# A fused attention and MLP kernel: the order of MLP units in the gaps between attention bursts, and the start of the first four units

## The chip, the cores and the metric

The kernel runs on one core of one Trainium2 chip. A core has TensorE (PE, matmuls), ScalarE (ACT), VectorE (DVE), GpSimd (POOL) and SyncE (SP, which here only issues transfers). Matmul results lie in PSUM, operands in SBUF, inputs and outputs in device memory. The metric is the device time of one launch in microseconds; lower is better.

## The reference

Attention with normalised queries and keys over 8 batches, 12 heads, 448 positions and 64 values per head; then a two-layer MLP (768 to 2048 to 768) over the 3,584 tokens with a leaky activation that has one slope per hidden column:

```python
def rmsnorm(x, g):
    return x / sqrt(mean(x * x, axis=-1) + 1e-06) * g
scores = (rmsnorm(q, g_q) @ rmsnorm(k, g_k).T) / sqrt(64)
attn = exp(scores - max(scores))
attn = attn / (sum(attn) + 1e-09)
x = (attn @ v) with the heads side by side        # 3584 x 768
h = x @ w_in
g = maximum(h, 0) + alpha * minimum(h, 0)
out = g @ w_out
```

The kernel takes a constant bias of -8 in the exponent in place of the maximum. It computes the activation as the larger of `h` and `alpha * h`, which is the same for slopes between 0 and 1.

## The kernel before

**Tiles and stages.** The unit of attention is a group `y` of four heads; a batch has three (G = 3), so there are 24. Its work in order:

- `load_qk` brings q and k into `nat` (on SP, from six buffers, so three groups); `square` (on POOL from group 2), `reduce` (DVE, tile `ss`), `root` (ACT, a logarithm and an exponential, tile `rr`) and `scale` (POOL, and DVE for a few, tile `qs`) normalise them.
- `turn` puts head values on the partitions: on PE through the tile `tps` for groups below 8, with DVE copies to `qT` and `kT`; from group 8 a transposing DMA does it, and `turn` is one DVE multiplication.
- `score` is four 64 by 64 matmuls into a tile `sc` of two PSUM banks (pool `pss`, two tiles). `soft` is an ACT exponential of the tile (1.0 us alone, about 0.94 in a row) into `expT`. Seven of each make a group.
- `den` sums the exponentials in 28 matmuls (tile `dn`); `log` and `invert` on ACT make the inverse (`rden`); `attv` takes 28 matmuls with the values (`av`), and a DVE multiplication writes one third of the batch's `xT`. `dn` and `av` share the pool `psa`, one tile with the tag `acc`.

The MLP is cut into units. `up(b, ft)` makes 128 of the 2,048 hidden columns of a batch: six matmuls over two halves of three thirds of `xT`, then ACT writes `ah` (alpha times h) and DVE the larger of both to `gT`. `down(b0, t, oh)` makes half of the output columns of 128 tokens of a pair of batches: 16 matmuls over all `gT`, a DVE copy to `osb`, and, after the second half, two output transfers on SP. Both write single banks of `psf` (two banks, tag `mm`), or half of the `acc` tile when `spare` is set. `spin(count)` gives PE matmuls whose result nobody reads.

**Order.** Every engine works in the order in which the program issues; the code writes that order. A small planner (lines 335 to 435) divides the work into 66 bursts of two or three score tiles. `dens` and `avs` say in which burst a group's denominators and values stand, `turn_at` where it is turned, `roots` where it is normalised, and `prep`, `post` and `jobs` where loads, squares and reduces stand. The MLP units of a batch are spread over the next batch's bursts (`gaps`), by a running sum of assumed costs (1.13 us for `up`, 2.6 for `down`); `old` are `down` units carried over, `new` those of this pair of batches.

Before, unit order in a gap is: the first of a burst from `old` while there is one, then `up`, and at the end `new`. One unit per burst, behind the first, may use the spare tile. The first MLP units stand in burst 12, together with the values of group 2, after a burst 11 with its denominators:

```python
        lead = n in (den_at[G - 1], av_at[G - 1])
        if lead and n in dens:
            den(dens[n])
            log(dens[n])
            invert(dens[n])
        elif lead:
            attv(avs[n])
```

`spin` fills PE ahead of the first units: after the scores in bursts 0, 1, 3 and 10, and in bursts 11 and 12. The weights come on POOL's queue: `w_in` in four parts in bursts 0 to 6, `w_out` in four parts, one each in bursts 10 to 13.

Of the kernel before, what the change touches and what calls it, by code (L numbers as in the profile page):

```python
# [9 lines left out]
FP32 = mybir.dt.float32  # L10
# [11 lines left out]
def kernel(  # L22
# [12 lines left out]
    nc = tc.nc  # L35

    B, H, S, D = q.shape
# [193 lines left out]
            scale=QK_SCALE, bias=expb[:, 0:1],  # L231
        )

    def over_keys(name, y, weights):
        acc = psa.tile([128, 2, 512], FP32, name=name, tag="acc")
        e = expT[y]
        for j in range(J):
            for g in range(2):
                for par in range(2):
                    nc.tensor.matmul(  # L240
                        out=acc[ds(64 * par, 64), g, :S],
                        lhsT=weights(g, par, j),
                        rhs=e[ds(64 * g, 64), j, par, :],
                        start=(j == 0),
                        stop=(j == J - 1),
                    )
        return acc
# [11 lines left out]
        r = rden[y]  # L259
        nc.scalar.activation(out=r, in_=r, func=AF.Exp, scale=-1.0)  # L260

    def attv(y):
        b, i = divmod(y, G)
        vv = vt[b]
        av = over_keys("av", y, lambda g, par, j: vv[ds(64 * g, 64), 2 * i + par, j, :])
        if i == 0:
            xT[b] = att.tile([128, 2, G, S], FP16, name="xT", tag="xT")
        nc.vector.tensor_mul(  # L268
            out=xT[b][:, :, i, :], in0=av[:, :, :S], in1=rden[y]
        )  # L270


    def bank(name, spare):
# [2 lines left out]
            return t[:, 0]  # L276
        return psf.tile([128, 512], FP32, name=name, tag="mm")

    def up(b, ft, spare=False):
        x = xT[b].rearrange("p g i c -> p (g i) c")  # L280
        hT = bank("hT", spare)
        order = [g * G + i for i in range(G) for g in range(2)]
        for c in order:
            nc.tensor.matmul(  # L284
                out=hT[:, :S],
                lhsT=w_in_sb[:, c, ts(ft, 128)],
                rhs=x[:, c, :],
                start=(c == order[0]),
                stop=(c == order[-1]),
            )  # L290
        ah = ffn.tile([128, S], FP16, name="ah", tag="ah", bufs=3)
        nc.scalar.activation(out=ah, in_=hT[:, :S], func=AF.Copy, scale=alpha_sb[:, ft : ft + 1])  # L292
        nc.vector.tensor_max(out=gT[:, ft, ds((b & 1) * S, S)], in0=hT[:, :S], in1=ah)  # L293
# [43 lines left out]
    while m < NG * J or len(avs) < NG:  # L337
        n = len(bursts)
        if len(dens) > len(avs):
            avs[n] = len(avs)  # L340
        elif len(dens) < NG and last_in.get(len(dens), n) < n:
            dens[n] = len(dens)
        wide = n in dens and dens[n] >= G or n in avs and avs[n] >= G
        count = min(3 if wide else 2, NG * J - m)
        bursts.append([divmod(m + c, J) for c in range(count)])
        for y, j in bursts[n]:
            first_in.setdefault(y, n)
            if j == J - 1:
                last_in[y] = n
        m += count  # L350
# [11 lines left out]
    turn_at = {  # L362
        y: max(n for n in range(first_in[y]) if n not in dens) for y in range(1, NG)
    }
    turn_at[2] = av_at[0] + 1
    turns = {n: y for y, n in turn_at.items()}
    jobs = {}
    for y in range(G, NG):

        early = y < G + 2  # L370
        n = turn_at[y - 1] if early else max(d for d in dens if d <= turn_at[y] - 2)
        at(n - (8 if early else 5), load_qk, y)
        for nm in "qk":
            (after if early else at)(n - 2, square, y, nm)
            if early:
                after(n, reduce, y, nm)
            else:
                jobs.setdefault(n, []).append((reduce, (y, nm)))
        roots[n + 1] = y
    for b in range(1, B):  # L380
        at(av_at[G * b] - 4, load_v, b)

# [2 lines left out]

    periods, carry = [], []
    for b in range(B):
        ups = [(UP, up, (b, ft)) for ft in range(NF)]
        odd = b % 2
        new = [  # L390
            (DOWN, down, (b - odd, t, oh))
            for t in (range(3, J) if odd else range(3)) for oh in range(2)
        ]
        tail = len(new) if b == B - 1 else 2 if odd or b == 0 else 1
        periods.append((ups, carry, new[:tail]))
        carry = new[tail:]

    def cost(n):
        return (
            0.31 + 0.19 * len(bursts[n])  # L400
            + (1.35 if n in dens or n in avs else 0.0) + (0.9 if turns.get(n, TD) < TD else 0.0)
        )

    first = av_at[G - 1]
    gaps = [[] for _ in range(NB)]
    for b in range(B - 1):
        lo, hi = av_at[G * b + G - 1], av_at[G * b + 2 * G - 1]
        ups, old, new = (list(u) for u in periods[b])
        mlp = sum(u[0] for u in ups + old + new)
        per = (mlp + sum(cost(n) for n in range(lo, hi))) / (hi - lo)  # L410
        clock = 0.0
        for n in range(lo, hi):
            clock += cost(n)
            free = True
            while ups or old or new:
                if old and (free or not ups):
                    u = old.pop(0)
                elif ups:
                    u = ups.pop(0)
                else:  # L420
# [63 lines left out]
    for n in range(NB):  # L484
# [13 lines left out]
        plain = n not in dens and n not in avs  # L498
        wait = plain and gaps[n] and gaps[n][0][0] is up
        if lead and n in avs:  # L500
            spin(3)
        for t in tiles[:1] if wait else tiles[:2]:
            soft(*t)
        if n in dens and not lead:
# [21 lines left out]
                late = [(1, invert, (dens[n],))]  # L526
        done = 0

        spare_at, clock = None, 0.0
        for k, (f, a) in enumerate(gaps[n][:-1]):  # L530
            free = 2.3 if n in dens else 1.2 if n in avs else 0.1
            if spare_at is None and clock >= free and not turns.get(n, TD) < TD:
                spare_at = k
            clock += DOWN if f is down else UP
        for k, (f, a) in enumerate(gaps[n]):
            spare = k == spare_at
# [53 lines left out]
```

## Time and profile before

| What | us |
|---|---|
| Median of 9 runs | 453.92 |
| Lowest and highest | 453.13 and 456.49 |
| The profiled execution, its time | 455.64 |
| Span of its records | 453.9 |
| PE, ACT, DVE, POOL busy | 427.6, 290.0, 207.8, 171.1 |
| First matmul of the MLP starts | 48.30 |

The profile is one execution. Its page gives busy time of each engine, the span in 40 slices, the transfers, the chain of work that ended last and the costliest groups of instructions. A group's line names the code line, the engine, the operation, the tile written and those read, the count, the busy time and the mean of one. Other views list who waited for whom, sum up stretches of time, or give the instructions in order of time; a bracket in the last gives the idle time of the engine ahead and what ended it.

### The profile page before, as it was taken

The numbers are of one execution on the slowest core, as the hardware profiler recorded it, in microseconds if no ns is written. First come the engines' busy times: TensorE is split into PE (matmuls) and PEld (weight loads), VectorE is DVE, ScalarE is ACT, GpSimd is POOL, SyncE is SP. The second block draws the span as 40 slices with busy tenths as digits, with TensorE's granted clock in tenths as the row PEclk, the third lists the DMA queues.
The fourth block names the chain that finished last, engine by engine and source line by source line (L and its number), as shares of the span: only waits on it lengthen the run. The fifth ranks groups of instructions, "written<-read, shape, count | busy, mean of one in ns | idle before, by whom it ended". The sixth has DMA issues, their size and how long they took to land.

```text
span 453.9 us, 9099 instructions
## 1 busy us (share of the span) xinstructions
PE 427.6 (94%) x3848; PEld 230.1 (51%) x3848; DVE 207.8 (46%) x297; ACT 290.0 (64%) x401; POOL 171.1 (38%) x125
## 2 busy tenths in 40 slices
PE   6768989899999999999999999999999999999996
PEld 2333444455445555455545555455545555455563
DVE  2755454735364545345454535345564333343421
ACT  4997888568676757648786758658785847423300
POOL 4779944660570550750571450750541100000000
PEclk9998999999999999999999999999999999999999
DMA  8999995294657633665656632674352410111122
GB/s 190 228 239 242 236 241 119 34 177 124 141 79 158 157 76 83 109 159 143 135 106 136 157 82 77 114 162 136 77 92 46 77 37 1 35 36 36 35 71 69
DMA packets 60009, 52.77 MB, mean 116 GB/s; under 512 B 32688, under 2 KB 56512, under 8 KB 59968
## 3 DMA queue, kind: packets, MB, share of 16 engines
q1 hardware_dynamic: 47424, 39.27, 36.5%
q0 software_dynamic: 11808, 11.81, 16.6%
q10 hardware_dynamic: 736, 1.11, 1.0%
q8 instruction: 30, 0.49, 0.5%
q14 instruction: 11, 0.09, 0.1%
HBM read 45.62 MB, written 11.01 MB: 125 GB/s over the span
## 4 chain that ended last, share of the span: by engine, by line
PE 79%; ACT 14%; DVE 4%; DMA 1%; issue 1%; SPq 0%; ACTq 0%
PE op L301 31%; PE hT L284 18%; PE hTa L284 9%; ACT expT L229 8%; PE sc L217 7%; PE av L240 5%; PE dn L240 5%; ACT ah L292 2%; PE opa L301 2%; ACT rden L255 2%; DVE gT L293 2%; DMA nat<-in_k_dram 1%; ACT rden L260 1%; PE tps L193 1%; DVE ss L141 1%
## 5 line engine op out<-in xcount | busy, mean ns | idle before, releaser
L229 ACT ACTIVATE expT<-sc,expb 128x896 f16<-128x896 f32 x168 | 157.6, 1008 | 19.0 <-PE sc L217 18.8
L301 PE MATMUL op<-w_out_sb,gT 128*128 128x384 f16 x848 | 145.9, 326 | 2.1 <-DVE gT L293 2.0
L158 POOL TENSOR_TENSOR qs<-nat,rr 128x896 f16<-128x896 f32 x44 | 78.3, 1799 | 180.3 <-issue 159.0
L284 PE MATMUL hT<-xT,w_in_sb 128*128 128x448 f16 x558 | 117.1, 353 | 2.7 <-DVE gT L293 2.6
L301 PEld LDWEIGHTS <-gT 128*128 128x128 f16 x896 | 84.6, 98 | 65.5 <-issue 12.3
L284 PEld LDWEIGHTS <-w_in_sb 128*128 128x128 f16 x768 | 73.7, 98 | 72.8 <-issue 8.5
L292 ACT ACTIVATE ah<-hT,cols 128x448 f16<-128x448 f32 x93 | 59.1, 636 | 59.5 <-PE hT L284 59.3
L293 DVE TENSOR_TENSOR gT<-hT,ah 128x448 f16<-128x448 f32 x93 | 58.0, 624 | 76.5 <-ACT ah L292 76.5
L135 POOL TENSOR_TENSOR sq<-nat 128x896 f32<-128x896 f32 x44 | 73.0, 1681 | 1.0 <-DMA nat<-in_q_dram 1.0
L313 DVE COPY osb<-op 128x384 f32<-128x384 f32 x53 | 29.5, 557 | 89.4 <-PE op L301 89.4
L217 PE MATMUL sc<-qT,kT 64*64 64x448 f16 x672 | 53.4, 360 | 9.6 <-ACT expT L229 6.0
L292 ACT ACTIVATE ah<-hTa,cols 128x448 f16<-128x448 f32 x35 | 22.2, 633 | 49.5 <-PE hTa L284 49.5
L141 DVE TENSOR_REDUCE ss<-sq 128x14 f32<-128x896 f32 x48 | 49.9, 1077 | 7.2 <-ACT sq L133 6.8
L284 PE MATMUL hTa<-xT,w_in_sb 128*128 128x448 f16 x210 | 45.4, 352 | 0.0
L217 PEld LDWEIGHTS <-kT 64*64 64x64 f16 x672 | 19.2, 104 | 39.1 <-issue 29.0
L240 PE MATMUL av<-expT,vt 64*64 64x448 f16 x672 | 36.0, 350 | 2.2 <-ACT rden L255 2.2
L240 PE MATMUL dn<-expT,ones 64*64 64x448 f16 x672 | 36.6, 354 | 0.2 <-DVE gT L293 0.2
L268 DVE TENSOR_TENSOR xT<-av,rden 128x896 f16<-128x896 f32 x24 | 26.2, 1090 | 22.3 <-PE av L240 22.3
L293 DVE TENSOR_TENSOR gT<-hTa,ah 128x448 f16<-128x448 f32 x35 | 21.8, 623 | 31.3 <-ACT ah L292 31.3
L240 PEld LDWEIGHTS <-vt 64*64 64x64 f16 x672 | 20.3, 107 | 14.3 <-issue 3.7
L240 PEld LDWEIGHTS <-ones 64*64 64x64 f16 x672 | 20.7, 108 | 12.7 <-issue 2.1
L255 ACT ACTIVATE rden<-dn 128x896 f32<-128x896 f32 x24 | 22.3, 930 | 2.9 <-PE dn L240 2.9
(37 smaller groups left out, 134.4 us busy)
## 6 DMA issues: line engine op xcount, KB each, us to landing
out_dram<-osb SPq DMA_DIRECT2D x54, 192.0 KB, 2.7
nat<-in_q_dram SPq DMA_DIRECT2D x46, 224.0 KB, 5.8
nat<-in_k_dram SPq DMA_DIRECT2D x46, 224.0 KB, 6.9
vt<-in_v_dram POOLq DMA_DIRECT2D x16, 336.0 KB, 7.3
w_in_sb<-in_moe_w_in_dram POOLq DMA_DIRECT2D x4, 768.0 KB, 13.4
w_out_sb<-in_moe_w_out_dram POOLq DMA_DIRECT2D x4, 768.0 KB, 15.6
nat<-in_q_dram ACTq DMA_DIRECT2D x2, 224.0 KB, 4.6
nat<-in_k_dram ACTq DMA_DIRECT2D x2, 224.0 KB, 6.7
```

What stands on the lines that cost most here:

```text
L135: nc.gpsimd.tensor_mul(out=sqf, in0=src, in1=src)
L141: nc.vector.tensor_reduce(out=ss_t[y][:, "qk".index(nm)].rearrange("p h j -> p (h j)").unsqueeze(2), in_=sqs[y, nm], axis=AXIS_X, op=ALU.add,)
L158: eng.tensor_mul(out=t.rearrange("p j h d -> p h j d"), in0=nat[y, nm], in1=rr_t[y][:, "qk".index(nm)].unsqueeze(3).broadcast_to((128, 2, ...
L217: nc.tensor.matmul(out=sc[ds(64 * g, 64), par, :S].rearrange("p (j c) -> p j c", j=J), lhsT=kT[ds(64 * par, 64), j, g, :], rhs=qT[ds(64 * ...
L229: nc.scalar.activation(out=expT[y][:, j], in_=scs[y, j][:, :, :S], func=AF.Exp, scale=QK_SCALE, bias=expb[:, 0:1],)
L240: nc.tensor.matmul(out=acc[ds(64 * par, 64), g, :S], lhsT=weights(g, par, j), rhs=e[ds(64 * g, 64), j, par, :], start=(j == 0), stop=(j == ...
L255: nc.scalar.activation(out=r, in_=rden[y][:, :, :S], func=AF.Ln)
L284: nc.tensor.matmul(out=hT[:, :S], lhsT=w_in_sb[:, c, ts(ft, 128)], rhs=x[:, c, :], start=(c == order[0]), stop=(c == order[-1]),)
L292: nc.scalar.activation(out=ah, in_=hT[:, :S], func=AF.Copy, scale=alpha_sb[:, ft : ft + 1])
L293: nc.vector.tensor_max(out=gT[:, ft, ds((b & 1) * S, S)], in0=hT[:, :S], in1=ah)
L301: nc.tensor.matmul(out=op[:, :OH], lhsT=gT[:, ft, ts(t, 128)], rhs=w_out_sb[:, ft, ds(oh * OH, OH)], start=(ft == 0), stop=(ft == NF - 1),)
L313: nc.vector.tensor_copy(out=o[:, ds(oh * OH, OH)], in_=op[:, :OH])
```

## The change

Five things change, all in the order of work or in the PSUM tiles.

1. The values of group 2 move from burst 12 into burst 11, directly behind its denominators, and go to a score tile (`spare`), while the logarithm and the inverse are issued between its matmuls and the multiplication. MLP units start in burst 11.
2. Units 0 to 3 of batch 0 are cut in two. `begin` sums the first two thirds of `xT`: unit 0 in burst 10 between its scores, 1 to 3 in burst 11 around the scores; 2 and 3 lie in the halves of the `acc` tile (`hTb`). `up` then adds the last third. The `spin` calls of bursts 10, 11 and 12 go; burst 6 gets one, as it no longer has a turn.
3. Group 2 is turned in burst 5, behind the values of group 0, instead of in burst 6; group 4 is normalised in burst 11 instead of 10. The `w_out` parts move one burst earlier each.
4. In a gap, carried `down` units stand first only in bursts with denominators or values (`wide`) as long as there are enough of those; other bursts get `up` units. Batch 0 takes four of its `down` units in its own period instead of two. In the plan that results, bursts 16 to 18 hold four `down` units of batch 0 (before, burst 18 holds two, and burst 16 has `up` units); bursts 31, 46 and 61 hold six `up` units each; and bursts 34, 49 and 64, which before have `up` units and then a `down` of the new pair, hold two `down` units, the carried one first.
5. Every third unit behind the first free place may use the spare tile, where before one per burst could. A PE turn stands behind the second unit of a burst where the burst has more than two.

```diff
-    def over_keys(name, y, weights):
-        acc = psa.tile([128, 2, 512], FP32, name=name, tag="acc")
+    def over_keys(name, y, weights, spare=False):
+        pool, tag = (pss, "sc") if spare else (psa, "acc")
+        acc = pool.tile([128, 2, 512], FP32, name=name, tag=tag)
...
-    def attv(y):
+    def attv(y, spare=False, jobs=()):
         b, i = divmod(y, G)
         vv = vt[b]
-        av = over_keys("av", y, lambda g, par, j: vv[ds(64 * g, 64), 2 * i + par, j, :])
+        av = over_keys(
+            "av", y, lambda g, par, j: vv[ds(64 * g, 64), 2 * i + par, j, :], spare
+        )
+        for f in jobs:
+            f(y)
...
+    begun = {}
+
+    def up_part(hT, b, ft, lo, hi):
+
+        for i in range(lo, hi):
+            for g in range(2):
+                nc.tensor.matmul(
+                    out=hT[:, :S],
+                    lhsT=w_in_sb[:, g * G + i, ts(ft, 128)],
+                    rhs=xT[b][:, g, i, :],
+                    start=(i == 0 and g == 0),
+                    stop=(i == G - 1 and g == 1),
+                )
+
+    def begin(ft):
+
+        if ft < 2:
+            begun[ft] = bank("hT", False)
+        elif ft == 2:
+            t = psa.tile([128, 2, 512], FP32, name="hTb", tag="acc")
+            begun[2], begun[3] = t[:, 0], t[:, 1]
+        up_part(begun[ft], 0, ft, 0, G - 1)
+
     def up(b, ft, spare=False):
...
+        early = b == 0 and ft in begun
+        hT = begun[ft] if early else bank("hT", spare)
+        up_part(hT, b, ft, G - 1 if early else 0, G)
...
             dens[n] = len(dens)
-        wide = n in dens and dens[n] >= G or n in avs and avs[n] >= G
-        count = min(3 if wide else 2, NG * J - m)
+            if dens[n] == G - 1:
+                avs[n] = G - 1
+        three = n in dens and dens[n] >= G or n in avs and avs[n] >= G
+        count = min(3 if three else 2, NG * J - m)
...
-    turn_at[2] = av_at[0] + 1
+    turn_at[2] = av_at[0]
...
-        n = turn_at[y - 1] if early else max(d for d in dens if d <= turn_at[y] - 2)
+        n = turn_at[y - 1] + (y == G) if early else max(d for d in dens if d <= turn_at[y] - 2)
...
-        roots[n + 1] = y
+        roots[n + 1 + (y == G + 1)] = y
...
-        ups = [(UP, up, (b, ft)) for ft in range(NF)]
+        ups = [(UP / 3 if b == 0 and ft < 4 else UP, up, (b, ft)) for ft in range(NF)]
...
-        tail = len(new) if b == B - 1 else 2 if odd or b == 0 else 1
+        tail = len(new) if b == B - 1 else 4 if b == 0 else 2 if odd else 1
...
+    def wide(n):
+        return n in dens or n in avs
...
-                if old and (free or not ups):
+                if old and (not ups or free and (
+                    wide(n) or len(old) > sum(wide(c) for c in range(n, hi))
+                )):
                     u = old.pop(0)
...
-        lead = n in (den_at[G - 1], av_at[G - 1])
-        if lead and n in dens:
+        lead = n == den_at[G - 1]
+        if lead:
             den(dens[n])
-            log(dens[n])
-            invert(dens[n])
-        elif lead:
-            attv(avs[n])
+            attv(avs[n], True, (log, invert))
         for t in tiles[:2]:
             score(*t)
-        plain = n not in dens and n not in avs
-        wait = plain and gaps[n] and gaps[n][0][0] is up
-        if lead and n in avs:
-            spin(3)
+            if lead and t == tiles[0]:
+                begin(1)
+                begin(2)
+            elif n == den_at[G - 1] - 1 and t == tiles[0]:
+                begin(0)
+        plain = lead or n not in dens and n not in avs
+        wait = plain and not lead and gaps[n] and gaps[n][0][0] is up
+        if lead:
+            begin(3)
...
-            if spare_at is None and clock >= free and not turns.get(n, TD) < TD:
-                spare_at = k
+            if clock >= free and not turns.get(n, TD) < TD and (
+                not spare_at or k - spare_at[-1] > 2
+            ):
+                spare_at.append(k)
...
-            if k == 0 and n in turns:
+            if n in turns and k == (
+                0 if turns[n] >= TD or plain else max(min(1, len(gaps[n]) - 2), 0)
+            ):
                 turn(turns[n])
...
-        if n < first and plain and n not in turns:
+        if n < den_at[G - 1] - 1 and plain and n not in turns:
             spin(4)
-        elif lead and n in dens:
-            spin(8)
```

More of the change, by code (lines that the diff above doesn't have):

```diff
@@ L277, in bank @@
         return psf.tile([128, 512], FP32, name=name, tag="mm")
-    def up(b, ft, spare=False):
[L280 to L290, printed above, removed]
+    begun = {}
[16 more added lines that the diff above has]
+        up_part(begun[ft], 0, ft, 0, G - 1)
+    def up(b, ft, spare=False):
+        early = b == 0 and ft in begun
+        hT = begun[ft] if early else bank("hT", spare)
+        up_part(hT, b, ft, G - 1 if early else 0, G)
         ah = ffn.tile([128, S], FP16, name="ah", tag="ah", bufs=3)
@@ L527 @@
         done = 0
-        spare_at, clock = None, 0.0
+        spare_at, clock = [], 0.0
         for k, (f, a) in enumerate(gaps[n][:-1]):
             free = 2.3 if n in dens else 1.2 if n in avs else 0.1
-            if spare_at is None and clock >= free and not turns.get(n, TD) < TD:
-                spare_at = k
+            if clock >= free and not turns.get(n, TD) < TD and (
+                not spare_at or k - spare_at[-1] > 2
+            ):
+                spare_at.append(k)
             clock += DOWN if f is down else UP
         for k, (f, a) in enumerate(gaps[n]):
-            spare = k == spare_at
+            spare = k in spare_at
             if f is down:
```

## The prediction

> **What bounds the kernel now.** I read the page's busy table and slices first, then windows by stage, then the waits, then the timeline of the stretch that the diff rewrites.
>
> ```profile
> PE 427.6 (94%) x3848; PEld 230.1 (51%) x3848; DVE 207.8 (46%) x297; ACT 290.0 (64%) x401; POOL 171.1 (38%) x125
> ...
> PE   6768989899999999999999999999999999999996
> ...
> PEclk9998999999999999999999999999999999999999
> DMA  8999995294657633665656632674352410111122
> ```
>
> TensorE (PE) sets the end; its idle slices are nearly all in the first eight (a slice is 11.35 us). One slice has a reduced clock. DMA is full for six slices, to about 70 us.
>
> ```profile
> 24.00:39.80 15.80, 9.98 (x157) 5.60 (x157) 9.32 (x11) 14.38 (x20) 14.07 (x9) 0.99 1.18 234
> 39.80:48.30 8.50, 8.34 (x92) 3.66 (x88) 4.63 (x5) 6.16 (x9) 8.48 (x8) 0.82 1.17 250
> 48.30:87.50 39.20, 36.26 (x347) 19.36 (x345) 20.07 (x29) 29.49 (x43) 22.25 (x16) 1.00 0.74 158
> 87.50:135.30 47.80, 44.42 (x431) 23.39 (x430) 23.58 (x33) 35.45 (x49) 24.83 (x18) 1.00 0.64 128
> 135.30:450.00 314.70, 311.13 (x2689) 169.92 (x2688) 138.88 (x204) 187.87 (x259) 87.31 (x57) 1.00 0.43 94
> ```
>
> Columns: stretch, length, then PE, weight loads, DVE, ACT, POOL. To 39.8 ACT is the limit (14.38 of 15.80). From 39.8 to 48.3 PE looks full, ACT is not (6.16 of 8.50), and the clock is 0.82. Then PE leaves 2.9 us idle to 87.5, 3.4 to 135.3, 3.6 in the remaining 315.
>
> ```profile
> 39.78 1.67 PE L328 MATMUL spin<-idle,ident 128*128 128x448 f16 x4
> 41.39 2.22 PE L240 MATMUL dn<-expT,ones 64*64 64x448 f16 x28
> 43.66 0.92 ACT L255 ACTIVATE rden<-dn 128x896 f32<-128x896 f32 x1 [1.80 <-PE dn L240]
> 43.92 1.69 PE L328 MATMUL spin<-idle,ident 128*128 128x448 f16 x8
> 45.53 1.52 PE L240 MATMUL av<-expT,vt 64*64 64x448 f16 x28
> 47.17 1.09 DVE L268 TENSOR_TENSOR xT<-av,rden 128x896 f16<-128x896 f32 x1 [3.72 <-PE av L240]
> 47.72 0.74 PE L328 MATMUL spin<-idle,ident 128*128 128x448 f16 x3
> ```
>
> The "full" PE is partly idle work: 15 spin matmuls. The denominators took 2.22 us at half clock against 1.49 to 1.52 elsewhere. Values come only after the logarithm, so the first MLP matmul is at 48.30.
>
> ```profile
> 187.79 2.44 PE L284 MATMUL hT<-xT,w_in_sb 128*128 128x448 f16 x12
> 191.25 0.97 PE L301 MATMUL op<-w_out_sb,gT 128*128 128x384 f16 x5 [1.01 <-DVE gT L293]
> ```
>
> Here `down` directly follows the last two `up` units and waits for what they write.
>
> [...] The records have a half-clock window, 39.44 to 42.85, but the window before it held some 1.8 us of matmuls, [...] The trace shows about 0.1 us per change (from a `down`'s first matmul to the next instruction group it is 2.69 us where scores follow, 2.61 where an `up` does); the change keeps nearly all of these. [...] w_out parts take 15.6 us to land in the full stretch.
>
> **The change, part by part.** Prices: `up` 1.14 us (six matmuls), `down` 2.61, denominators or values 1.32, two score tiles 0.4; exponential 0.94 in a row; ah 0.64; gT 0.62; a root pair 0.55; logarithm 0.92; inverse 0.95; xT 1.09; reduce 1.04.
>
> *Turn of unit 2 one burst earlier.* It then stands behind the values of unit 0 (end 26.9) instead of behind burst 6's scores (28.44). Its k part needs POOL's scale, which ends at 27.16. kT ends at about 29.3 instead of 30.25, and the 0.88 us that ACT idled at 30.75 for scores goes. Worth 0.9 us, as ACT is the limit there.
>
> *Burst 10 to 12.* Spins: 15 removed here, four added in burst 6, where PE idles. Unit 2's values go straight behind its denominators into a score tile, and four `up` units begin on the two finished thirds of xT (4 of 6 matmuls, 0.75 us each). With the 0.9: first part 37.3 to 38.05, inside the wait for kT (0.99 idle before); denominators 38.75 to 40.1, full clock; values to 41.45; log 40.3 to 41.2; inverse to 42.15; xT 42.25 to 43.3. The second score of burst 11 needs the values' tile and waits for that xT: 43.35. Third begin to 44.4. The four remainders (0.38 each) end at 45.9. Before, none of these four was complete until 49.5.
>
> *A wait that the change adds.* Unit 5's reduces now stand behind five gT on DVE. ACT: exponential to 44.7, root to 45.25, four ah to 47.8, the fifth 47.95 to 48.6; gT to 49.3; two reduces to 51.4. Root 5 is in ACT's queue ahead of ah 5, the next exponential and ah 6 to 8, so ACT stands from 49.55 to 51.4, and `up` 8 waits for a bank to 53.25: 1.7 us on PE. Before, these reduces ended by 43.5 with no MLP on DVE.
>
> *Bursts 13 to 18, by the same walk.* Burst 13's scores 54.4, burst 14's 59.9; burst 15: scores 64.2, values to 65.95, 1.55 waiting for an exponential, turn 5 behind xT at 70.4 (both waits are there before, 0.79 and 1.12), `up` 15 to 72.4. Then two `down` per pair of bursts: 73.0 first `down`, burst 19's first score at about 88.2. Before, that score is at 87.51 with 16 `up` and two `down` done; now four `down` are done: 2 x 2.61 - 0.7 = 4.5 us ahead.
>
> *Weights.* The last quarter of w_out is issued at about 52 instead of 55.9 and needed at the 13th matmul of the first `down`, 75. Before it landed at 71.83. All loads are the same bytes, so nothing, with 3 us of cover. But POOL now issues three w_out parts and two v loads in a row ahead of unit 4's scales, which end about 49 instead of 46.45; turn 4 needs them at 56.7, so nothing again.
>
> *Batch 1 (bursts 19 to 26).* Fewer `down` are left, so ACT comes close: bursts 22 to 25 need 20.9 us of PE and 21.8 of ACT (11 exponentials, 9 ah, two log pairs, two roots). Walked with two banks: `up` 7 waits 1.1, `up` 10 1.5, `up` 13 0.6; before, bursts 24 and 25 lose 0.85, 0.32 and 0.77, plus some hidden in the stream, 2.4 in all. Of the 4.5 about 0.6 is given back: 3.9.
>
> *Later batches.* `down` first in bursts 34 and 49 removes a wait of 1.1 (1.01 in the lines above) twice; in burst 64 about 0.55. The spare tile for every third unit removes about 0.4 each in bursts 31 and 46, and moving three units in a row without it to 36 and 51 gives it back. Sum 2.75. The new place of the PE turns changes nothing: bursts 15, 18 and 20 have two units, for which the rule gives index 0, and burst 13 is plain. Rest list and end are untouched.
>
> Sum 3.9 + 2.75 = 6.65 us. The profiled execution took 455.64 with a span of 453.9, so 1.7 lies around it: span 447.25, time 449.0. But it is 1.72 above the median of the runs, which gives 447.3 if the median run has the same half-clock window. I take 448.0 between the two.
>
> **Rivals.** (B) *ACT gives back more.* From 48.3 to 87.5 ACT idles only 9.7 us and my walk spends over half. In-order waits like root 5's, one more per burst in bursts 11 to 15 and 22 to 25, would cost 0.4 each, 3.6: 451.6. For it: ACT interleaves three kinds of work there; against: the walk has them in order. (C) *Half clock again.* [...] 1.6 us a window (0.85 on the spins, 0.75 on the denominators before), 449.6 with one. [...] (D) *Hidden anyway*: the early start only lengthens waits at turn 5 and `down`, the later 2.75 remaining: 451.2. (E) *Slower: the last quarter of w_out.* If five issues in a row block POOL until earlier parts land, squares, scales and the last w_out issue all slip. Each us past 75 is a us on PE; it decides at 75 + 6.65 + 1.4 = about 83. Landing takes 16.2 at most, so an issue at 67 would be needed; two w_in issues in a row did not block. (F) The benefit is larger: bursts 11 to 15 overlap better, root 5's wait absent: 446.
>
> **How the numbers follow.** A measurement can tell about 0.3%, 1.36 us: faster below 452.56, slower above 455.28. Chances: forecast 0.48 (446.3 to 449.5), F 0.10, C 0.12, B 0.12, D 0.08, E or several waits together 0.10 of which 0.07 passes 455.28. Faster takes forecast, F, C, most of B and D: 0.86; same 0.07; slower 0.07. The range leaves out the top of E, part of B and D, and the best of F: 445.0 to 451.8.
>
> **What would show it.** Right: denominators and values of unit 2 adjoining near 39 to 41.5; first complete gT near 46; ACT idle before root 5 by about 1.8 us, released by DVE; burst 19 after four `down` near 88; no PE wait for gT ahead of `down` at bursts 34 and 49. Wrong: `down` waiting on the w_out load, a second 0.5 clock stretch, PE waits for gT above 3 us in batch 1, or ACT idle for scores after 45.

## The result, and the profile after

The changed kernel takes 449.68 us (median; 449.44 to 450.10), the kernel before, run beside it on the same chips, 453.76 us. The ratio is 0.9904, 95% interval 0.9889 to 0.9918: faster by about 4.1 us, or 1.0%. The forecast was 448.0 with a range of 445.0 to 451.8.

The profiled execution after the change took 449.5 us with a span of 447.7. Its busy table and slices (each digit a tenth of a slice of 11.2 us):

```profile
PE 424.6 (95%) x3837; PEld 229.3 (51%) x3837; DVE 207.7 (46%) x297; ACT 290.4 (65%) x401; POOL 171.2 (38%) x125
...
PE   8779798989889999999999999999999999999996
...
PEclk9999999999999999999999999999999999999999
DMA  8999995285547651883666651872362501111122
```

Three things differ from before. TensorE loses 3.0 us of busy time, which is spin matmuls and matmuls at the reduced clock, not work. The slice with the reduced clock is gone. And slices 11 and 12 of TensorE (from 112 to 134 us) stand at 8, because units of batch 1 wait there.

The same windows by stage, after (length, then busy PE, weight loads, DVE, ACT, POOL; clock; transfer share; GB/s):

```profile
24.00:39.80 15.80, 12.97 (x200) 7.48 (x203) 10.49 (x12) 14.94 (x19) 15.45 (x10) 1.00 1.17 244
39.80:48.30 8.50, 6.68 (x55) 3.02 (x46) 3.09 (x5) 6.08 (x10) 8.30 (x9) 1.00 1.18 237
48.30:87.50 39.20, 35.93 (x356) 19.59 (x356) 21.00 (x30) 28.23 (x40) 20.87 (x14) 1.00 0.75 163
87.50:135.30 47.80, 43.14 (x437) 22.58 (x438) 24.35 (x34) 36.28 (x51) 25.49 (x18) 1.00 0.61 128
```

From 87.5 to 135.3 TensorE is now idle for 4.7 us where it was 3.4. That is where part of the gain goes. Here are its three waits in batch 1 (bursts 23, 24 and 26; start, length, instruction; in brackets the idle time ahead and what ended it), and then the two that stood there before (the second profile of the kernel before, from the first experiment below):

```profile
113.98 1.29 PE L290 MATMUL hT<-xT,w_in_sb 128*128 128x448 f16 x6 [0.67 <-DVE gT L313]
...
120.68 1.30 PE L290 MATMUL hT<-xT,w_in_sb 128*128 128x448 f16 x6 [1.01 <-DVE gT L313]
...
128.02 0.38 PE L217 MATMUL sc<-qT,kT 64*64 64x448 f16 x4 [1.34 <-DVE kT L179]
```

```profile
118.91 2.65 PE L284 MATMUL hT<-xT,w_in_sb 128*128 128x448 f16 x12 [0.85 <-DVE gT L293]
...
126.72 1.29 PE L284 MATMUL hT<-xT,w_in_sb 128*128 128x448 f16 x6 [0.76 <-DVE gT L293]
```

The timeline of the start, after:

```profile
37.93 1.49 PE L241 MATMUL dn<-expT,ones 64*64 64x448 f16 x28
...
39.25 1.49 PE L241 MATMUL av<-expT,vt 64*64 64x448 f16 x28
39.48 0.92 ACT L256 ACTIVATE rden<-dn 128x896 f32<-128x896 f32 x1 [0.31 <-PE dn L241]
...
41.41 1.09 DVE L273 TENSOR_TENSOR xT<-av,rden 128x896 f16<-128x896 f32 x1 [1.76 <-ACT rden L261]
...
45.01 1.16 DVE L313 TENSOR_TENSOR gT<-hT,ah 128x448 f16<-128x448 f32 x2 [2.51 <-ACT ah L312]
...
46.75 0.54 PE L290 MATMUL hTb<-xT,w_in_sb 128*128 128x448 f16 x2 [1.82 <-DVE gT L313]
```

Denominators and values adjoin, at a granted clock of 1.00, and the first two `gT` are written by 46.2. The last line is a wait that the forecast did not have. A little later, ACT's timeline of the changed kernel:

```profile
49.05 1.00 ACT L229 ACTIVATE expT<-sc,expb 128x896 f16<-128x896 f32 x1
51.83 0.32 ACT L152 ACTIVATE rr<-ss,epsb 128x28 f32<-128x28 f32 x1 [1.78 <-DVE ss L141]
52.18 0.23 ACT L153 ACTIVATE rr<-rr 128x28 f32<-128x28 f32 x1
52.31 0.62 ACT L312 ACTIVATE ah<-hT,cols 128x448 f16<-128x448 f32 x1
```

This is root 5 in ACT's queue, waiting for the reduces that stand behind five `gT` on DVE. It was forecast, and it holds up an `up` unit on TensorE for 1.20 us at 53.64. The waits view of the new kernel, three lines of it (who waited for whom: total, times, longest):

```profile
PE hT L290 <- DVE gT L313: 3.5, 6, 1.2
...
PE hTb L290 <- DVE gT L313: 1.8, 1, 1.8
...
PE sc L217 <- DVE kT L179: 1.3, 1, 1.3
```

And burst 34, where `down` waited 1.01 us before, is one stream of two `down` units (the first of the 32 matmuls lies ahead of this view):

```profile
183.74 5.20 PE L321 MATMUL op<-w_out_sb,gT 128*128 128x384 f16 x31
```

**Where the 4 us come from.** Times from the start of the span shift with the first loads (ACT's wait for the first k tile was 1.84 us in the first profile of before and 0.78 after), so stretches are compared from one common event: the first matmul of the values of group 0, at 24.15 to 25.79 us in the profiles used here. The work up to there is the same in all of them, so this spread is not an effect of any edit. The rows give the time from there to the first score of a burst, or to the end of the records. At bursts 28, 35, 50 and the end, all kernels have done the same work; at burst 19 the kernel marked with a star has done two `down` (5.22 us) more than before; at burst 13 it has done nine `up` units, the kernel before three, so its larger figure there is not a loss. "Before, again" is the unchanged kernel in the second profile that the first experiment gives.

| us from the values of group 0 to | burst 13 | burst 19 | burst 28 | burst 35 | burst 50 | end |
|---|---|---|---|---|---|---|
| before, first profile | 26.85 | 62.16 | 117.31 | 168.59 | 270.18 | 428.52 |
| before, again | 25.27 | 60.57 | 115.72 | 167.00 | 268.59 | 426.92 |
| after * | 30.33 | 63.25 | 114.63 | 164.34 | 264.92 | 423.19 |

Against "before, again", the change has 5.22 - 2.68 = 2.54 us in hand at burst 19 and 1.09 at burst 28: batch 1 gives back 1.45. It then gains 1.57 to burst 35 and 1.01 to burst 50, and 0.06 to the end: 3.73 in all. The profiled pair that the forecast started from shows more, 453.9 - 447.7 = 6.2 us of span, because the first profile of before has 1.6 us more in the same stretch and came to the common event 0.81 us later (25.35 against 24.54).

### The profile page after: what moved, and what is told of

It reads as the page before. It is cut to its first block, busy times and chain, and to the rows that moved or that the text cites. A ratio compares the mean times of both kernels' runs of the same rounds, so it can differ in the third digit from the quotient of the medians.

```text
span 447.7 us, 9084 instructions
## 1 busy us (share of the span) xinstructions
PE 424.6 (95%) x3837; PEld 229.3 (51%) x3837; DVE 207.7 (46%) x297; ACT 290.4 (65%) x401; POOL 171.2 (38%) x125
## 4 chain that ended last, share of the span: by engine, by line
PE 81%; ACT 11%; DVE 5%; DMA 1%; issue 1%; ACTq 0%
PE op L321 32%; PE hT L290 18%; PE hTa L290 9%; PE sc L217 7%; ACT expT L229 6%; PE dn L241 6%; PE av L241 6%; ACT ah L312 2%; PE opa L321 2%; DVE gT L313 2%; PE tps L193 1%; DMA nat<-in_k_dram 1%; DVE ss L141 1%; ACT rden L256 1%; ACT rden L261 1%
## 5 line engine op out<-in xcount | busy, mean ns | idle before, releaser
L290 PE MATMUL hT<-xT,w_in_sb 128*128 128x448 f16 x528 | 112.1, 353 | 3.5 <-DVE gT L313 3.5
L312 ACT ACTIVATE ah<-hT,cols 128x448 f16<-128x448 f32 x88 | 55.7, 634 | 62.9 <-PE hT L290 62.7
L313 DVE TENSOR_TENSOR gT<-hT,ah 128x448 f16<-128x448 f32 x88 | 54.8, 624 | 61.3 <-ACT ah L312 61.2
L290 PE MATMUL hTa<-xT,w_in_sb 128*128 128x448 f16 x228 | 49.3, 352 | 0.0
L312 ACT ACTIVATE ah<-hTa,cols 128x448 f16<-128x448 f32 x38 | 24.1, 633 | 37.6 <-PE hTa L290 37.6
L313 DVE TENSOR_TENSOR gT<-hTa,ah 128x448 f16<-128x448 f32 x38 | 23.7, 625 | 33.8 <-ACT ah L312 33.8
L261 ACT ACTIVATE rden<-rden 128x896 f32<-128x896 f32 x24 | 22.9, 953 | 0.7
```

The source lines that it names most:

```text
L290: nc.tensor.matmul(out=hT[:, :S], lhsT=w_in_sb[:, g * G + i, ts(ft, 128)], rhs=xT[b][:, g, i, :], start=(i == 0 and g == 0), stop=(i == G ...
```

## The experiments

The question was which of the five parts earns the time, and where the rest of the forecast 6 us went. The theory was the forecast's: a sum of local gains, about 4 us by the early start together with the four `down` units up to burst 19, and 2.75 us by the order later on. The rivals were the half clock, a hidden early start, and queueing behind DVE or the transfers.

### The kernel before, unchanged

> The kernel before, unchanged, to see the granted clock of many executions beside their times. If the half-clock window of the profiled execution (39.44 to 42.85 us) is what set it 1.9 us above the median of 453.76, then executions with a mean clock of 1.0 take about 453.3 and those with one window near burst 10 or 11 about 455 to 456.5, and the gain over a usual execution is 4.1 although the two profiled ones differ by 6.2. Rival: the window costs nothing in the end (ACT or the transfers set the pace there); then times do not go with the clock, and the 1.9 us lie around the span.

Measured: 453.68 us, ratio 1.0001 (0.999 to 1.0012); the profiled execution took 453.39 with a span of 451.6. Its timeline at the denominators and values of group 2:

```profile
39.85 1.52 PE L240 MATMUL dn<-expT,ones 64*64 64x448 f16 x28
41.42 0.92 ACT L255 ACTIVATE rden<-dn 128x896 f32<-128x896 f32 x1 [0.21 <-PE dn L240]
43.30 1.52 PE L240 MATMUL av<-expT,vt 64*64 64x448 f16 x28
...
46.06 2.43 PE L284 MATMUL hT<-xT,w_in_sb 128*128 128x448 f16 x12
```

The denominators take 1.52 us, not 2.22, and the MLP starts at 46.06, not 48.30. So the granted clock of 0.50 that I had seen here (39.44 to 42.85) belongs to that execution and not to every execution of the program. It cost 1.6 us (62.16 - 60.57); the rest of the difference between the two profiles is the start, 25.35 against 24.70. The clocks of the 22 executions of this run say the same. Eleven have a mean granted clock of 0.999 or more and take 453.28 to 454.09 us (median 453.43); seven at 0.995 or 0.996 take 453.30 to 455.25; four at 0.991 or 0.992 take 454.81 to 456.26. So times do go with the clock in this run, and against the median of the eleven an execution took from nothing to 1.8 us more at 0.995 or 0.996, and 1.4 to 2.8 more at 0.991 or 0.992. Such stretches lift the median of this kernel by about 0.3 us, not by the 1.6 of the first profile. The changed kernel at a mean clock of 1.000 takes 449.50 to 449.98 us (median 449.69): at full clock the gain is about 3.7 us, as in the table above.

### The early start alone, with the unit order of before

Parts 1, 2, 3 and 5 stay; with this order no burst has a second spare place.

```diff
-        tail = len(new) if b == B - 1 else 4 if b == 0 else 2 if odd else 1
+        tail = len(new) if b == B - 1 else 2 if odd or b == 0 else 1
...
-                if old and (not ups or free and (
-                    wide(n) or len(old) > sum(wide(c) for c in range(n, hi))
-                )):
+                if old and (free or not ups):
```

> Parts 1, 2, 3 and 5 of the change with the unit order of before. My account: the early start is worth about 3 us over a usual execution by burst 19, and the later waits of before (bursts 24, 25, 34, 49, 64) stay: 450.8, ratio 0.9935. Rival, the early start is hidden (ACT limits bursts 11 to 16, so that what starts early waits later) and nearly all of the gain is in the order: 453 or more, ratio over 0.998.

Measured: 453.24 us, ratio 0.9985 (0.9971 to 0.9999), almost nothing. From the values of group 0 it needs 60.36 us to burst 19 and 426.74 to the end, 0.2 less than before at both. The expectation fell. TensorE's timeline of this kernel shows what stands where the early start should have shown:

```profile
54.40 0.38 PE L217 MATMUL sc<-qT,kT 64*64 64x448 f16 x4 [1.13 <-ACT expT L229]
...
65.18 1.51 PE L241 MATMUL av<-expT,vt 64*64 64x448 f16 x26 [1.38 <-DMA vt<-in_v_dram]
...
85.41 0.57 PE L217 MATMUL sc<-qT,kT 64*64 64x448 f16 x8 [1.31 <-DVE kT L204]
```

TensorE comes sooner to an exponential, to the values of batch 1 and to the `kT` of burst 19, and waits there: 3.8 us in these three, where the kernel before, in its second profile, waits for two exponentials (0.79 each) and a turn (1.12), 2.7 us. With the smaller ones and the 1.82 us that `hTb` costs here too, the lead is gone. My reading is that starting early pays only if there is TensorE work that needs none of these; the new order in batch 0 alone, below, puts it to the test.

### The new unit order alone

The kernel before with only the two edits above in the other direction (the `wide` rule and four `down` units of batch 0 in its own period); the late start and one spare place stay.

> Part 4 of the change alone: the order of units, with the start of before and one spare place per burst. My account: the waits at bursts 34, 49 and 64 go (2.75 us), but the runs of six units in bursts 31, 46 and 61 have one spare place and lose about 0.9 us each, and batch 1 loses about as much as it gains: 453.5, ratio 0.9995. Rival, the order is worth its 2.75 us by itself: 451.0, ratio 0.994.

Measured: 453.27 us, ratio 0.9989 (0.9976 to 1.0001). From the values of group 0 to the end: 426.56 us, 0.36 less than before. TensorE no longer waits for `gT` ahead of a `down`, and from burst 28 to 35 it takes 50.11 us against 51.28. But it is 1.06 us late at burst 28. At burst 19 it is still 0.40 ahead (counting the two `down` that it has done more); batch 1, with less `down` work carried into it, then takes 1.46 away, by the same three waits that the changed kernel has (0.67, 1.02 and 1.34 us here). So the loss in batch 1 is the price of the new order, with or without the early start.

So the parts are not additive: 0.2 and 0.4 us alone, 3.7 together. The next two experiments show where the difference lies.

### The new order in batch 0 only

```diff
-                    wide(n) or len(old) > sum(wide(c) for c in range(n, hi))
+                    b > 0 or wide(n) or len(old) > sum(wide(c) for c in range(n, hi))
```

> The changed kernel with the unit order of before from batch 1 on; batch 0 keeps the new order with four of its second-layer units in bursts 16 to 18. My account: the early start is worth something only where units that need no ACT fill the PE time that it frees, so here it is worth about 2.5 us by burst 19 although the early start alone brought 0.6 and the order alone 0.5; the later waits stay: 451.5, ratio 0.995. Rival, the parts simply add up: 453.0 or more, ratio over 0.998.

Measured: 453.53 us, ratio 0.9989 (0.9979 to 0.9999). The expectation was right up to burst 19 and fell behind it. Up to there the kernel is the changed one to the hundredth (63.25 us), so it has the 2.54 us in hand, where the start alone has 0.21 and the order alone 0.40: with `down` units to do, the early start pays. It then loses 1.04 us against it to burst 28 (115.67 against 114.63), 1.57 more to burst 35 and 1.01 to burst 50. In batch 1 TensorE waits for `gT` or `kT` four times (1.01, 0.76, 1.01, 1.34), in the changed kernel three times (0.67, 1.01, 1.34): the difference of 1.1 us is the 1.04. The 2.54 us in hand at burst 19 are thus spent in batch 1, down to 0.05. With the new order there as well, where carried `down` units are kept for the bursts with denominators and values, 1.09 are left. The later batches' 2.6 us come from that order too (with its second spare place, next), and not from the start: here both waits of 1.0 us ahead of `down` are back.

### One spare place per burst

```diff
-                not spare_at or k - spare_at[-1] > 2
+                not spare_at
```

> The changed kernel with one spare place per burst instead of every third unit; only bursts 31, 46 and 61 have a second one in the changed plan. My account: unit 10 of each waits for a bank as in burst 24 of before (0.85 us and some in the stream): 2.5 us in all, 452.2, ratio to before 0.9965. Rival, the banks are not short there, because each of those bursts holds only two exponentials: 449.7 to 450.3, ratio 0.991 to 0.9925.

Measured: 451.02 us, ratio 0.9928 (0.9903 to 0.9953). By the trace it loses 0.42 us by burst 35, 0.83 by burst 50 and 1.24 at the end (424.43 against 423.19): 0.42 in each of the three bursts with six `up` units. The second spare place is worth 1.2 us; the 0.85 per burst expected here were twice too much, and the prediction's 0.4 was right.

With this the parts can be put together, as us in hand over "before, again" (at burst 19 with 5.22 added for kernels that have done two `down` more):

| us in hand at | burst 19 | burst 28 | end |
|---|---|---|---|
| early start alone | 0.21 | 0.21 | 0.18 |
| new order alone | 0.40 | -1.06 | 0.36 |
| new order in batch 0 only | 2.54 | 0.05 | 0.04 |
| changed, one spare place | 2.53 | 1.06 | 2.49 |
| changed | 2.54 | 1.09 | 3.73 |

Of the 3.2 us by which the whole exceeds its two parts, 1.9 arise up to burst 19, where early start and extra `down` units need each other, and 1.2 are the second spare place, which the early start alone has no burst for and the order alone does not have.

### The turn of unit 2 at its old place

```diff
-    turn_at[2] = av_at[0]
+    turn_at[2] = av_at[0] + 1
...
-        n = turn_at[y - 1] + (y == G) if early else max(d for d in dens if d <= turn_at[y] - 2)
+        n = turn_at[y - 1] if early else max(d for d in dens if d <= turn_at[y] - 2)
```

> The changed kernel with group 2 turned in burst 6 again, its normalisation as before. The prediction: 0.9 us slower than the changed kernel, as ACT is the limit there: 450.6, ratio to before 0.993. Rival, the loss is made good where ACT has room before burst 11, or by the transfers that set the pace to 70 us: 449.7 to 450.0, ratio 0.991 to 0.9915.

Measured: 450.50 us, ratio 0.9925 (0.9908 to 0.9942); 423.99 us to the end, 0.80 more than the changed kernel, and 0.80 more already at burst 11. ACT's timeline of this kernel, and then of the changed one:

```profile
27.40 1.91 ACT L229 ACTIVATE expT<-sc,expb 128x896 f16<-128x896 f32 x2
30.19 1.90 ACT L229 ACTIVATE expT<-sc,expb 128x896 f16<-128x896 f32 x2 [0.88 <-PE sc L217]
```

```profile
27.34 3.70 ACT L229 ACTIVATE expT<-sc,expb 128x896 f16<-128x896 f32 x4
```

Four exponentials in a row, or two, a gap of 0.88 and two. Here ACT is the limit, and its gap goes through to the end almost whole (0.80 of 0.88). This is the cleanest step of the change.

### The two last thirds in one tile, together

Units 2 and 3 lie in the two halves of one tile (`hTb`). In the changed kernel TensorE wrote the last third of unit 3 only when DVE had written the `gT` of unit 2 (the 1.82 us above), although they lie in different halves: in the order of the program, ACT and DVE read the tile in between. Here the last thirds of both are issued ahead of these reads:

```diff
-        up_part(hT, b, ft, G - 1 if early else 0, G)
+        if not (early and ft == 3):
+            up_part(hT, b, ft, G - 1 if early else 0, G)
+        if early and ft == 2:
+            up_part(begun[3], b, 3, G - 1, G)
```

> The changed kernel with the last thirds of units 2 and 3 issued together, ahead of what ACT and DVE do for unit 2; they share the tile hTb, and in the changed kernel unit 3's last third waits 1.82 us for unit 2's gT. If this wait sets the pace: burst 12 starts about 1.5 us earlier, 448.2, ratio 0.988. Rival, ACT and the wait of root 5 stand behind it anyway: 449.4 to 449.9, ratio 0.9905 to 0.9915.

Measured: 448.61 us, ratio 0.9877 (0.9853 to 0.9901); 421.93 us to the end, 1.26 less than the changed kernel. TensorE's timeline of this kernel:

```profile
45.29 1.29 PE L290 MATMUL hT<-xT,w_in_sb 128*128 128x448 f16 x6 [0.37 <-DVE gT L316]
...
51.99 1.29 PE L290 MATMUL hT<-xT,w_in_sb 128*128 128x448 f16 x6 [1.39 <-DVE gT L316]
```

With this order the wait of 1.82 is gone, the unit behind waits 0.37 for a bank instead, and the bank wait behind root 5 has grown from 1.20 to 1.39: of 1.45 us freed, 1.26 arrive.

### The reduces of unit 5 ahead of the `gT` of burst 11

```diff
+        for f, a in jobs.pop(n, []) if lead else []:
+            f(*a)
         done = 0
```

> The changed kernel with unit group 5's two reduces issued ahead of burst 11's gT on DVE, not behind them. If root 5 (1.78 us of ACT, then 1.20 of PE for a bank) sets the pace: 448.3, ratio 0.988. Rival, the time is taken back at burst 15, where turn 5 waits for xT and scores for exponentials: 449.3 to 449.9, ratio 0.990 to 0.9915.

Measured: 448.55 us, ratio 0.9874 (0.9847 to 0.9901); 1.37 us earlier at burst 13 and 1.33 at the end. On ACT root 5 starts at 50.52 without a wait, and TensorE's bank wait of 1.20 is gone. So the forecast wait of root 5 was real, and avoidable. Its length on ACT was right (1.85 forecast, 1.78 measured), its price on TensorE was put too high: 1.7 forecast, 1.20 of wait and 1.33 to the end measured. TensorE waits 1.57 us for the values of batch 1 here (at 65.59), but that costs next to nothing, since it takes the place of the waits for an exponential and a turn that the changed kernel has just behind (0.79 and 1.12, here 0 and 0.17).

### Both, and then what they lay bare

> Both at once. If the two waits are one behind the other on ACT and PE, they add up: 446.9, ratio 0.985. If they are two faces of one limit (ACT has as much work as bursts 11 to 15 have time), both bring what one brings: 448.3, ratio 0.988.

Measured, with both edits: 447.28 us, ratio 0.986 (0.9826 to 0.9894); 420.20 to the end, 2.99 less than the changed kernel. The sum of the two alone is 1.26 + 1.33 = 2.59, so they add up. With four runs from 446.31 to 450.26 the median says less than the profile does. A wait for the values of batch 1 stands in this kernel too:

```profile
62.95 1.51 PE L241 MATMUL av<-expT,vt 64*64 64x448 f16 x26 [1.16 <-DMA vt<-in_v_dram]
```

The second half of the values of batch 1 landed at 62.90. In the changed kernel it landed at 62.73 and was needed at 64.66: 1.9 us to spare, which the forecast never worked out. It looked only at the weights.

The next kernel adds the gain of the later turns (one DVE multiplication, `kT` by `gain`) ahead of the units of its burst:

```diff
+        if turns.get(n, 0) >= TD:
+            turn(turns[n])
```

(the later places are then used for the PE turns alone).

> Both at once, and the DVE gain of turns from group 8 on stands ahead of its burst's units, not behind the first: the scores of group 9 in burst 26, which wait 1.34 us for it, should not. My account: 1.3 us under the run with both, 445.6 to 447.0, ratio 0.982 to 0.985. Rival, the gain now waits on DVE for the transposing transfer in other bursts and holds back gT and xT: as slow as the changed kernel or slower, 449.7 or more.

Measured: 448.4 us (446.55 to 450.69), ratio 0.9876 (0.9844 to 0.9908); not better. The transfer came later still in the profiled execution:

```profile
64.91 2.80 PE L241 MATMUL av<-expT,vt 64*64 64x448 f16 x26 [2.85 <-DMA vt<-in_v_dram]
```

Behind this gap the granted clock of that execution is 0.50 from 64.97 to 68.38 (the mean is 0.57 from 64.5 to 68.0 and 0.95 from there to 72.0), and the same 26 matmuls take 2.80 us instead of 1.51. By burst 19 it is 3.0 us behind the profile with both edits. And the wait that the edit was made for stayed as it was, 1.34 us. DVE's timeline in that kernel tells why:

```profile
123.29 2.07 DVE L141 TENSOR_REDUCE ss<-sq 128x14 f32<-128x896 f32 x2
125.28 1.08 DVE L273 TENSOR_TENSOR xT<-av,rden 128x896 f16<-128x896 f32 x1
126.28 1.76 DVE L179 TENSOR_SCALAR kT<-kT,gain 128x896 f16<-128x896 f16 x1
```

It moved the gain ahead of a `gT`, but the two reduces and the `xT` multiplication are issued before it still. And it then took 1.76 us itself.

### The values of batch 1 first

The load of batch 1's values goes ahead of the squares of unit 5 and of all parts of `w_out`, on top of the first two edits:

```diff
-    for b in range(1, B):
+    for b in range(2, B):
         at(av_at[G * b] - 4, load_v, b)
...
+    prep[first - 2].insert(0, (load_v, (1,)))
```

> The kernel with both repairs (units 2 and 3 together, unit 5's reduces first), and the value load of batch 1 issued on POOL's queue ahead of unit 5's squares and of all w_out parts instead of behind two of them. In the runs with both repairs its second half landed at 62.90 and 64.86 us and the values of unit 3 waited for it 1.16 and 2.85 us. If this load is what makes those kernels spread from 446.3 to 450.7, no wait on it is left and the runs lie within 1 us of 446.2, ratio 0.983. Rival, the last w_out part becomes late in its place (needed at about 72): PE waits there and the time stays at 447 to 448.5, ratio 0.986 or more.

Measured: 446.54 us (446.37 to 447.46), ratio 0.9839 (0.9821 to 0.9857). The values land at 51.52, the last part of `w_out` at 71.18, and TensorE waits for neither, though the second is close: the 13th matmul of the first `down`, which needs it, starts at 71.26. That rival was 0.1 us away. The profiled end is the same as with both edits alone (420.17 against 420.20 us): the waits for the exponential and the turn, 0.79 and 1.12, are back where 1.16 and 0.58 were. But the median is 0.7 lower, and the runs lie within 1.1 us where they spread over 4. With four and five runs that is a hint, not a proof, that the late load was a hazard from run to run rather than a fixed cost.

### The gain ahead of the `xT` multiplication

```diff
         if n in avs and not lead:
+            if turns.get(n, 0) >= TD:
+                turn(turns[n])
             attv(avs[n])
```

(and these turns are left out at the later places).

> The kernel of values_first with the gain of turns from group 8 on issued on DVE ahead of the multiplication that writes xT, where both stand in one burst. In burst 26 the scores of group 9 waited 1.34 us because reduces and xT stood ahead of the gain. If the order on DVE is the cause, that wait falls to 0.3 or less: 445.2, ratio 0.981. Rival, the next unit's bank or an exponential takes its place: no difference from values_first.

Measured: 445.42 us (444.94 to 445.7), ratio 0.9808 (0.9791 to 0.9825): the fastest kernel here, 4.3 us below the changed one. DVE's timeline at burst 25 in the changed kernel and in this one:

```profile
125.21 1.08 DVE L273 TENSOR_TENSOR xT<-av,rden 128x896 f16<-128x896 f32 x1
126.46 0.62 DVE L313 TENSOR_TENSOR gT<-hT,ah 128x448 f16<-128x448 f32 x1 [0.17 <-ACT ah L312]
127.00 0.97 DVE L179 TENSOR_SCALAR kT<-kT,gain 128x896 f16<-128x896 f16 x1
```

```profile
122.09 0.44 DVE L179 TENSOR_SCALAR kT<-kT,gain 128x896 f16<-128x896 f16 x1
122.45 1.08 DVE L273 TENSOR_TENSOR xT<-av,rden 128x896 f16<-128x896 f32 x1
123.45 1.14 DVE L316 TENSOR_TENSOR gT<-hT,ah 128x448 f16<-128x448 f32 x2
```

The scores of burst 26 no longer wait 1.34 us for `kT`; a wait for a bank of 0.36 is what is left. At burst 28 the gain is 1.12 us (110.50 against 111.62), at the end 1.43 (418.74).

## Why the prediction was right, and where not

**The walk through bursts 10 to 19: its steps came, its clock times partly by luck.** Turn of unit 2: 0.9 forecast, 0.80 measured by undoing it. ACT's wait ahead of root 5: 1.85 forecast, 1.78 measured. Burst 14: 59.9 forecast, 59.87 measured. Burst 19: 88.2 with four `down`, measured 87.79. But the changed kernel's profile came to the values of group 0 0.81 us earlier than the profile that the walk started from. Counted from there, burst 14 was 0.78 us later than forecast and burst 19 0.40. The walk left out the wait for `hTb` (worth 1.26 us), and two waits that it put too high made up for it: the bank wait behind root 5 (1.7 forecast, 1.20 measured) and the exponential of burst 15 (1.55 forecast, 0.79 measured). The last part of `w_out` landed at 70.55, ahead of the first `down` at 72.26, so the weights cost nothing and rival E (the last quarter late) did not come.

**The later batches: right.** 2.75 us forecast, 1.57 + 1.01 + 0.06 = 2.64 measured. It is right in its parts too: from burst 28 to 42, 42 to 57 and 57 to the end the changed kernel gains 1.00, 1.01 and 0.63 us, where 1.1, 1.1 and 0.55 were forecast. Bursts 34 and 49 have no wait ahead of `down`. The spare places were forecast to balance, 0.4 us won in bursts 31 and 46 and given back from 36 and 51 on; 0.42 won per burst by the second place and, from burst 35 to 42, 0.57 given back were measured.

**The sum: too high, and the step to the median wrong.** 6.65 us were forecast from the profiled execution, and 6.2 of span came. But 0.81 of the 6.2 lie ahead of the values of group 0, where nothing was changed. From there on the pair differs by 5.33 us: the walk to burst 19 brought 4.1 instead of 4.5, batch 1 took 1.45 instead of 0.6, the later batches brought 2.64 instead of 2.75. The step that failed most is the last: "I take 448.0 between the two". It split the difference between a profiled execution and a median that differ by 1.7 us, as if half of the half-clock window were in the median. By the executions of the first experiment about 0.3 us are, so removing the window is worth no more than that to the median, and the better answer was the one from the profiled execution: 449.0 (measured 449.68). Rival C (a half-clock window in the new kernel, 449.6) names nearly the measured time but is not its cause: the profile has no such window, and the other executions at a mean clock of 1.000 take the same 449.65 to 449.98 us.

**Batch 1: mis-sized.** "Of the 4.5 about 0.6 is given back": 1.45 was. The waits after the change were nearly as walked, 3.2 forecast (1.1, 1.5, 0.6) and 3.02 measured (0.67, 1.01, 1.34). But the last of them is a wait for DVE's gain on `kT`, not for a bank. And for the kernel before I put the loss at 2.4, "some hidden in the stream"; the second profile has 0.85 + 0.76 = 1.61. The difference of what is measured, 1.41, is nearly the 1.45.

**Missed: two waits and a near miss with one shape.** The second half of `hTb` (1.82 us, worth 1.26), the gain on `kT` (1.34, worth 1.12 at burst 28) and the values of batch 1 (on time by 1.9) all stand behind something that I had not walked: reads of the other half of a tile, DVE's reduces, POOL's transfers. The step on `hTb` was "the four remainders (0.38 each) end at 45.9"; they end at 47.3. Of the transfers, I watched `down` on the `w_out` load; it was the neighbouring load that became late once other waits were mended.

**Rival D (hidden anyway): true of the early start alone.** It yields 0.2 us with the old order. That its trace has these waits is shown; which of them takes which share of the lead stays open, since none was removed there by itself.

## What to carry to other kernels

When a stage is started earlier, walk every queue that it passes, the transfers too, and ask for each next consumer whether its operand is there: here four things moved ahead (the second half of a shared tile, two reduces, a load, a gain) brought as much again, 4.3 us, as the change itself, 4.1, though the load's share is only a hint. Parts of a schedule change are not additive: two that give 0.2 and 0.4 us alone gave 3.7 together, as one makes TensorE early and the other keeps work for it to do, and as the second spare place serves only the new order. And before a forecast is set against a median, look whether the profiled execution is a usual one: the 1.6 us that a half-clock window cost in one profile here was about 0.3 us of the median.

## What was not expected of the hardware

- **The half clock came and went, and TensorE had not been idle throughout ahead of it.** The same program had a granted clock of 0.50 for 3.41 us (39.44 to 42.85) in one profile and none there in another. Three variants had such a stretch as well: from 11.10 to 17.92 us (one spare place, mean clock 0.990 over the execution), 13.98 to 17.40 (early start alone, 0.995) and 64.97 to 68.38 (behind the 2.85 us in which TensorE waited, 0.996); the first two lie ahead of the values of group 0 and so outside the comparisons above. In the 3.41 us ahead of these four, TensorE was busy for 1.90, 1.52, 1.76 and 0.56 us. What sets the half clock off is not shown.
- **The gain on DVE took longer where it overlapped POOL's scale.** The multiplication of 128 by 896 took 442 to 446 ns in all 16 places of the fastest kernel; in the one at burst 25, shown above, it ends at 122.53 and POOL's scale starts at 122.92. In the changed kernel 15 of 16 overlap POOL's scale and take 0.46 to 0.97 us, and the one that does not takes 443 ns; 1.76 us was the longest, in the variant shown above. All 16 that overlap, whenever they start, end about 0.25 us after the end of the scale instruction that was running. Why is not shown. My estimate from these numbers is that 0.53 us of the 1.34 us wait in burst 26 (0.97 against 0.44) went with POOL's scale, and that the order on DVE was the rest.
- **Transfers in a row on POOL's queue landed later, but did not hold POOL.** The third part of `w_out` needed 16.2 us from issue to landing before and 23.3 in the changed kernel, where it is the fifth of five transfers that are issued one behind the other (40.68 to 44.33); each issue took 0.7 to 0.8 us of POOL in both, and in the changed kernel POOL's next scale starts at 44.54, 0.20 us after the last issue.
